# Routed attention with a greedy expert layer: the first unit's values handled behind its queries, keys and scores

## The chip, the cores and the metric

The kernel runs on one core of a Trainium2 chip. The metric is the time of one execution in microseconds on the device; the median of several runs counts. One execution was also recorded by the hardware profiler, and all rows below come from it.

## What is computed

An attention that is routed by clusters feeds a layer of eight experts. Queries and keys are each given the nearest of 16 centroids of their head, a query sees only keys of its own cluster, and the result goes through a greedy assignment of tokens to experts with a fixed capacity.

```python
# q, k, v: 4 batches x 8 heads x 768 x 64, float32; centroids 8 x 16 x 64
q_assign = np.argmax(np.einsum('bhsd,hcd->bhsc', q_n, c_n), axis=-1)   # likewise k_assign
mask = q_assign[:, :, :, None] == k_assign[:, :, None, :]
scores = np.where(mask, scale * np.matmul(q, k.transpose(0, 1, 3, 2)), -1e9)
attn = softmax(scores)
x = np.matmul(attn, v)                       # 3072 tokens x 512
logits = x @ w_gate                          # 8 experts, at most 384 tokens each
# greedy: the largest logit first, each token to one expert
out[mask_e] = np.maximum(x[mask_e] @ w1[e], 0) @ w2[e]
```

## The kernel before

The attention is cut into 8 units (u = 0 to 7), each of four heads of one batch. A head has 768 tokens, that is 6 blocks of 128, so a unit has 24 blocks. Queries, keys and values are float32 and are worked on as two float16 parts, a high and a low one. A unit passes through these stages:

- `load` (L481) fetches q, k or v over the queue of SP into one of four buffers `ld`, in turn. Unit 0 fetches q and k head by head (192 KB each) and v whole (768 KB); all later units fetch everything whole. Unit 2's keys use the buffer that unit 0's values had.
- `split_sc` and `split_hi` (L628, L632) scale and form the high part on ACT, and `split_lo` (L636) forms the low part by a subtraction on POOL or DVE. `dup` (L643) copies high parts on ACT.
- `pt` and `ptc` (L724, L736) transpose by PE and copy the result out on DVE or ACT (unit 0), `trans` (L720) does it by a DMA (later units).
- `cent0` and `cent` (L700, L662) multiply by the centroids on PE, into a PSUM tile called `mx`. `hh0` to `hh3` and `hot0` to `hot3` (L667) find the nearest on DVE, `hh4`/`hot4` and `hh5`/`hot5` (L683) form and place the marks on DVE and ACT. In unit 0 this is done head by head (`hh`).
- `vs` (L746) sums v over the tokens with 12 products on PE, into `mx` as well; `vact` and `vh2` (L754, L757) read it on ACT and `vl2` (L760) on DVE. The result is used from `av,u,1` on.
- `m_mm` (L766) forms a block of scores on PE and `m_rd` (L773) takes its row maximum on DVE. `row0` and `row1` (L786, L790) turn the maxima into two more rows.
- `b_mm`, `b_exp`, `res` and `av` (L804 to L826) are the second pass: scores again, the exponential on ACT, its low part on POOL, and the product with v on PE.

`wd` (L657) is a dummy product on PE whose result nobody reads. The pool of `mx` holds one tile, so each user of `mx` waits until the last reader of the user before has finished. The expert stage follows the last unit.

The order of all this is written out by hand: `ATT_ORDER` (L21) is a text of 2037 steps, and each engine, and the queue of SP, takes its instructions in the order in which they stand there. The scheduler of the framework adds only the waits that the data need. Around the change the text read in turn: `load,0,v` as the third load, v's three split steps among those of heads 1 and 2, `vs,0` behind the marks of head 1, `vact,0`, `vh2,0` and `vl2,0` among the dummies that follow, and `load,2,k` in front of `load,1,v` and `load,1,q`.

Of the kernel before, what the change touches and what calls it, by code (L numbers as in the profile page):

```python
# [21 lines left out]
ident loadc load,0,q,0 wtio load,0,k,0 misc load,0,v,- load,0,q,1 c0 load,0,k,1 c1 load,0,q,2 c2,0 c2,1 load,0,k,2 c2,2
c2,3 load,0,q,3 c2,4 zqb c2,5 split_sc,0,q,0 loadg c2,6 c2,7 load,0,k,3 split_sc,0,k,0 c2,8 c2,9 zkb load,1,k,- c2,10
split_hi,0,q,0,P split_hi,0,k,0,P split_sc,0,q,1 c2,11 split_lo,0,q,0,P split_sc,0,k,1 split_hi,0,q,1,P c2,12 pt,0,qa,0
split_hi,0,k,1,P split_lo,0,k,0,P ptc,0,qa,0,D split_sc,0,v,- c2,13 pt,0,ka,0 split_lo,0,q,1,P ptc,0,ka,0,D
split_hi,0,v,-,P c2,14 pt,0,qa,1 split_lo,0,k,1,P ptc,0,qa,1,D c2,15 dup,0,q,0 pt,0,ka,1 wgs c3 dup,0,k,0 c4
split_lo,0,v,-,P ptc,0,ka,1,D split_sc,0,q,2 cent0,0,k cent0,0,q split_sc,0,k,2 wd wd hh0,0 split_hi,0,q,2,P wd wd hh1,0
wd wd split_hi,0,k,2,P wd hh2,0 wd wd dup,0,q,1 hh3,0 wd wd wd hh4,0,k dup,0,k,1 wd hh4,0,q wd split_lo,0,q,2,P
load,2,k,- hh5,0,k cent0,1,k hh5,0,q pt,0,kb,0 split_sc,0,q,3 split_lo,0,k,2,P pt,0,qb,0 ptc,0,kb,0,D cent0,1,q
ptc,0,qb,0,A pt,0,qa,2 zqm hh0,1 pt,0,ka,2 hh1,1 split_sc,0,k,3 m_mm,0,0 tab,8 hh2,1 tab,9 wd split_hi,0,q,3,P tab,10 wd  # L30
hh3,1 wd tab,11 wd tab,12 split_hi,0,k,3,P wd hh4,1,k split_lo,0,q,3,P wd hh4,1,q wd hh5,1,k ptc,0,qa,2,D vs,0 hh5,1,q
split_lo,0,k,3,P ptc,0,ka,2,A m_rd,0,0 load,1,v,- dup,0,q,2 tab,13 pt,0,kb,1 load,1,q,- tab,14 pt,0,qb,1 tab,15 tab,16
ptc,0,kb,1,A pt,0,qa,3 tab,17 ptc,0,qb,1,D tab,18 wd wd tab,19 dup,0,k,2 tab,20 ptc,0,qa,3,D pt,0,ka,3 tab,21 tab,34
m_mm,0,1 split_sc,1,k,- tab,0 ptc,0,ka,3,D m_mm,0,2 m_rd,0,1 m_mm,0,3 wd wd wd dup,0,q,3 m_rd,0,2 m_mm,0,4 dup,0,k,3 wd
wd wd split_hi,1,k,-,P m_rd,0,3 m_mm,0,5 wd wd wd m_rd,0,4 m_mm,0,6 wd vact,0 wd split_lo,1,k,-,P wd vh2,0 m_rd,0,5
m_mm,0,7 split_sc,1,q,- wd wd wd vl2,0 m_mm,0,8 row0,0,0 cent0,2,k row1,0,0 cent0,2,q m_rd,0,6 split_hi,1,q,-,P wd wd wd
hh0,2 pt,0,qm,0 trans,1,ka,- hh1,2 wd wd split_sc,1,v,- split_lo,1,q,-,P wd hh2,2 wd wd hh3,2 wd wd wd hh4,2,k wd
hh4,2,q wd m_rd,0,7 hh5,2,k cent0,3,k hh5,2,q cent0,3,q split_hi,1,v,-,P wd hh0,3 pt,0,kb,2 hh1,3 wd wd ptc,0,kb,2,D wd
wd trans,1,qa,- wd ptc,0,qm,0,A wd split_lo,1,v,-,P hh2,3 wd wd hh3,3 wd wd wd hh4,3,k wd wd hh4,3,q hh5,3,k wd m_rd,0,8
wd hh5,3,q wd wd wd cent,1,k,0 tab,1 pt,0,qb,2 tab,2 tab,3 pt,0,kb,3 tab,4 ptc,0,qb,2,A pt,0,qb,3 ptc,0,kb,3,D  # L40
cent,1,k,1 load,2,q,- cent,1,k,2 ptc,0,qb,3,A tab,5 load,2,v,- cent,1,k,3 tab,6 tab,7 load,3,k,- m_mm,0,9 hot0,1,k
dup,1,k,- tab,22 m_mm,0,10 tab,23 m_mm,0,11 hot1,1,k wd wd wd m_rd,0,9 wd wd dup,1,q,- wd wd wd hot2,1,k m_mm,0,12 wd wd
hot3,1,k wd split_hi,2,k,-,D wd wd m_rd,0,10 wd wd wd wd wd hot4,1,k b_mm,0,0 m_rd,0,11 hot5,1,k cent,1,q,0 cent,1,q,1
b_exp,0,0 trans,1,kb,- cent,1,q,2 row0,0,1 cent,1,q,3 row1,0,1 split_hi,2,q,-,D m_rd,0,12 res,0,0,P pt,0,qm,1 wd wd wd
hot0,1,q m_mm,0,13 b_mm,0,1 ptc,0,qm,1,A hot1,1,q av,0,0 hot2,1,q b_exp,0,1 m_mm,0,14 m_rd,0,13 split_hi,2,v,-,D
res,0,1,P hot3,1,q m_mm,0,15 b_mm,0,2 m_rd,0,14 av,0,1 b_exp,0,2 hot4,1,q m_mm,0,16 m_rd,0,15 hot5,1,q vs,1 res,0,2,P
dup,2,k,- trans,1,qb,- m_rd,0,16 m_mm,0,17 b_mm,0,3 m_rd,0,17 vact,1 m_mm,0,18 vh2,1 av,0,2 b_exp,0,3 row0,0,2 row1,0,2
b_mm,0,4 m_rd,0,18 res,0,3,P pt,0,qm,2 b_exp,0,4 vl2,1 m_mm,0,19 tab,24 ptc,0,qm,2,A m_rd,0,19 m_mm,0,20 res,0,4,P
av,0,3 b_mm,0,5 m_rd,0,20 m_mm,0,21 b_exp,0,5 av,0,4 split_lo,2,k,-,D b_mm,0,6 dup,2,q,- m_mm,0,22 m_rd,0,21 res,0,5,P
trans,2,ka,- b_exp,0,6 m_rd,0,22 m_mm,1,0 m_mm,0,23 res,0,6,P av,0,5 m_rd,1,0 b_mm,0,7 m_rd,0,23 m_mm,1,1 b_exp,0,7  # L50
row0,0,3 load,3,q,- b_mm,0,8 res,0,7,P row1,0,3 m_rd,1,1 pt,0,qm,3 b_exp,0,8 out0,0,0 m_mm,1,2 out1,0,0 ptc,0,qm,3,A
res,0,8,P b_mm,0,9 out2,0,0,D m_rd,1,2 cent,2,k,0 hi0,0,0 m_mm,1,3 b_exp,0,9 cent,2,k,1 hi1,0,0 b_mm,0,10
split_hi,3,k,-,D m_rd,1,3 res,0,9,P av,0,6 av,0,7 tab,25 tab,26 b_exp,0,10 m_mm,1,4 split_lo,2,q,-,D av,0,8 b_mm,0,11
m_mm,1,5 b_exp,0,11 av,0,9 m_rd,1,4 res,0,10,P trans,2,qa,- cent,2,k,2 cent,2,k,3 m_rd,1,5 b_mm,0,12 res,0,11,P m_mm,1,6
hot0,2,k b_exp,0,12 av,0,10 m_rd,1,6 b_mm,0,13 res,0,12,P m_mm,1,7 hot1,2,k b_exp,0,13 av,0,11 load,3,v,- m_rd,1,7
b_mm,0,14 res,0,13,P m_mm,1,8 out0,0,1 b_exp,0,14 b_mm,0,15 out1,0,1 out2,0,1,D res,0,14,P m_mm,1,9 m_rd,1,8 hi0,0,1
b_exp,0,15 hi1,0,1 b_mm,0,16 split_hi,3,q,-,D m_rd,1,9 res,0,15,P xtr,0,0 av,0,12 av,0,13 hot2,2,k b_exp,0,16 m_mm,1,10
split_lo,2,v,-,D xst,0,0 av,0,14 b_mm,0,17 m_mm,1,11 b_exp,0,17 m_rd,1,10 res,0,16,P av,0,15 load,4,k,- m_rd,1,11
b_mm,0,18 res,0,17,P m_mm,1,12 b_exp,0,18 row0,1,0 av,0,16 row1,1,0 m_rd,1,12 rowt,1,0 b_mm,0,19 res,0,18,P m_mm,1,13
hot3,2,k b_exp,0,19 av,0,17 m_rd,1,13 b_mm,0,20 res,0,19,P m_mm,1,14 out0,0,2 b_exp,0,20 out1,0,2 b_mm,0,21 out2,0,2,D  # L60
row2,1,0 res,0,20,P m_mm,1,15 m_rd,1,14 hi0,0,2 b_exp,0,21 hi1,0,2 b_mm,0,22 m_rd,1,15 res,0,21,P av,0,18 b_exp,0,22
av,0,19 hot4,2,k m_mm,1,16 res,0,22,P tab,27 hot5,2,k tab,28 lg0,0,0 m_rd,1,16 av,0,20 trans,2,kb,- b_mm,0,23 lg1,0,0
split_lo,3,k,-,D m_mm,1,17 b_exp,0,23 cent,2,q,0 cent,2,q,1 cent,2,q,2 cent,2,q,3 m_rd,1,17 res,0,23,P av,0,21 b_mm,1,0
hot0,2,q trans,3,ka,- m_mm,1,18 b_exp,1,0 av,0,22 hot1,2,q b_mm,1,1 hot2,2,q res,1,0,P m_mm,1,19 m_rd,1,18 b_exp,1,1
av,0,23 hot3,2,q dup,3,k,- b_mm,1,2 res,1,1,P hot4,2,q m_mm,1,20 load,4,q,- m_rd,1,19 vs,2 hot5,2,q b_exp,1,2
trans,2,qb,- out0,0,3 out1,0,3 out2,0,3,D b_mm,1,3 vact,2 res,1,2,P m_rd,1,20 hi0,0,3 m_mm,1,21 b_exp,1,3 hi1,0,3
# [1393 lines left out]
```

## Time and profile before

| | |
|---|---|
| median of three runs | 711.02 us (708.17 to 711.4) |
| the profiled execution | 707.99 us, of which the span of the trace is 706.2 |
| PE busy (share of the span) | 659.0 us (93%) |
| DVE busy | 525.8 us (74%) |
| ACT busy | 425.2 us (60%) |
| POOL busy | 500.7 us (71%) |

PE is TensorE, DVE is VectorE, ACT is ScalarE, POOL is GpSimd, SP is the engine whose queue issues the transfers. Dummy products count as busy PE. The attention takes about the first 400 us. A timeline row gives the start in us, the duration in us, the engine, the line of the kernel, the operation, the tile written and the tiles read, the shapes, how many neighbours of the same kind are merged, and in brackets how long the engine had been idle before it and what ended that.

### The profile page before, as it was taken

To read this page: it belongs to the slowest core of one execution; us is meant where nothing else is said; L and a number is where in the kernel's file an instruction comes from. 1 tells how busy PE (TensorE), PEld (TensorE's weight loads), DVE (VectorE), ACT (ScalarE), POOL (GpSimd) and SP (SyncE) were. 2 spreads that over 40 slices of the span, in tenths; PEclk is the share of its full clock that TensorE was granted. 3 is DMA by queue.
4 is the path that set the end of the run, shared out by engine and by line. 5 is a ranking of instruction groups with operands and counts; after the bars stand their busy time and mean duration, and the time that the engine had idled before them with its cause. 6 is when DMAs were issued, how large, how long until landed. Compare 5 with 4: busy or idle time off the path is not lost. (4 is left out here: it accounts for less than half of the span.)

```text
span 706.2 us, 19751 instructions
## 1 busy us (share of the span) xinstructions
PE 659.0 (93%) x8256; PEld 438.0 (62%) x8256; DVE 525.8 (74%) x1149; ACT 425.2 (60%) x554; POOL 500.7 (71%) x395
## 2 busy tenths in 40 slices
...
GB/s 184 165 237 136 172 140 190 138 175 157 153 202 164 126 132 96 171 93 92 19 35 49 69 3 255 143 215 205 169 304 103 295 135 254 180 335 217 33 13 45
DMA packets 175451, 105.85 MB, mean 150 GB/s; under 512 B 135426, under 2 KB 160002, under 8 KB 175362
## 3 DMA queue, kind: packets, MB, share of 16 engines
...
q8 instruction: 64, 1.05, 0.6%
...
HBM read 58.77 MB, written 12.58 MB: 101 GB/s over the span
## 5 line engine op out<-in xcount | busy, mean ns | idle before, releaser
L824 POOL TENSOR_TENSOR rt<-pt 128x768 f16<-128x768 f32 x180 | 280.6, 1573 | 75.9 <-ACT pt L816 72.4
L816 ACT ACTIVATE pt<-sc 128x768 f32<-128x768 f32 x192 | 154.4, 811 | 121.2 <-PE sc L813 112.7
L774 DVE TENSOR_REDUCE mxs<-sc 128x1 f32<-128x768 f32 x192 | 180.9, 950 | 23.4 <-PE sc L770 20.1
L1382 PE MATMUL pf<-xgt,w1h 128*128 128x384 f16 (+1 forms) x640 | 128.8, 294 | 0.0
L835 PE MATMUL av<-vh,pt 128*128 128x66 f16 x1152 | 125.4, 195 | 2.3 <-DVE xb L868 1.9
L838 PE MATMUL av<-vh,rt 128*128 128x66 f16 x1152 | 125.0, 194 | 1.4 <-POOL rt L824 1.4
L837 PE MATMUL av<-vl,pt 128*128 128x64 f16 x1152 | 125.0, 192 | 0.0
L837 PEld LDWEIGHTS <-pt 128*128 128x128 bf16 x1152 | 106.6, 99 | 13.0 <-issue 4.0
L835 PEld LDWEIGHTS <-pt 128*128 128x128 bf16 x1152 | 107.4, 98 | 10.0 <-issue 0.3
L838 PEld LDWEIGHTS <-rt 128*128 128x128 f16 x1152 | 106.2, 97 | 1.6 <-POOL rt L824 1.6
L809 PE MATMUL sc<-qbt,kbt 99*128 99x384 f16 x384 | 94.8, 328 | 9.5 <-DVE mxs L774 8.9
L770 PE MATMUL sc<-kbt,qbt 80*128 80x384 f16 x384 | 93.2, 326 | 4.1 <-DMA qbt<-qb 2.0
L813 PE MATMUL sc<-qat,kat 128*128 128x384 f16 x384 | 94.5, 327 | 0.0
L1382 PE MATMUL pf<-xgt,w1l 128*128 128x384 f16 (+1 forms) x320 | 90.0, 294 | 0.0
L1344 ACT ACTIVATE wr<-wr 128x1024 f32<-128x1024 f32 x64 | 66.7, 1046 | 26.8 <-PE pc L1300 23.3
L1382 PEld LDWEIGHTS <-w1h 128*128 128x128 f16 x640 | 57.3, 97 | 28.4 <-ACT w2h L1347 0.7
L1420 PE MATMUL pf<-w2h,hh 128*128 128x512 f16 x192 | 72.7, 378 | 0.0
L1420 PE MATMUL pf<-w2l,hh 128*128 128x512 f16 x192 | 72.5, 378 | 0.0
L1420 PE MATMUL pf<-w2h,hl 128*128 128x512 f16 x192 | 72.5, 378 | 0.0
L1354 POOL TENSOR_TENSOR w2l<-wr,w2h 128x1024 f16<-128x1024 f32 x32 | 67.7, 2132 | 1.5 <-ACT w2h L1347 1.1
L1354 POOL TENSOR_TENSOR w1l<-wr,w1h 128x1024 f16<-128x1024 f32 x32 | 67.5, 2139 | 0.2
...
## 6 DMA issues: line engine op xcount, KB each, us to landing
...
xg<-xrow,idx POOLq DMA_INDIRECT x24, 6.3
```

The lines of the kernel that those rows point to most:

```text
L770: nc.tensor.matmul(p[:, half, :S // 2], QBT[u][:D + C, i, :], KBT[u][:D + C, h * J + half * 3:h * J + half * 3 + 3, :], start=True, stop=True)
L774: nc.vector.tensor_reduce(mxs[u % 3][:, i:i + 1], MP.pop((u, i))[:, :, :S // 2], axis=AX.XY, op=OP.max)
L809: nc.tensor.matmul(ps[:, half, :S // 2], KBT[u][:ER + 3, s, :], QBT[u][:ER + 3, cs, :], start=True, stop=False)
L813: nc.tensor.matmul(ps[:, half, :S // 2], KAT[u][:, s, :], QAT[u][:, cs, :], start=False, stop=True)
L816: nc.scalar.activation(pts[(u * 12 + s // 2) % RP][:, s % 2], MP.pop((u, "b", s))[:, :, :S // 2], AF.Exp, scale=ESC)
L824: (nc.vector if e == "D" else nc.gpsimd).tensor_sub(rts[x][:, s % 2], p.rearrange("p a b -> p (a b)"), hi_view(pts[x])[:, s % 2])
L835: nc.tensor.matmul(o[:, j, :], hi[:, js], VH[u][:, s, :], start=(kt == 0 and j == 0), stop=False, skip_group_check=True)
L837: nc.tensor.matmul(o[:, j, :D], hi[:, js], VL[u][:, s, :], start=False, stop=False, skip_group_check=True)
L838: nc.tensor.matmul(o[:, j, :], r[:, js], VH[u][:, s, :], start=False, stop=(kt == J - 1), skip_group_check=True)
L1354: nc.gpsimd.tensor_sub(lo, wrs[c], hi)
L1382: nc.tensor.matmul(o, (w1l if i == 2 else w1h)[x][:, c, fs], xgt[x][:, h + int(i == 1), ts], start=(first and i == 0), stop=(last and i == ...
L1420: nc.tensor.matmul(PS["o", p, g], (hl if i == 2 else hh)[x][:, f, g * P:(g + 1) * P], (w2l if i == 1 else w2h)[x][:, f, :], start=(f == 0 ...
```

## The change

No instruction is added or taken away; 9 of the 2037 steps stand elsewhere. `load,0,v` goes from the third place among the loads to behind `load,0,k,3`. `split_sc,0,v` and `split_hi,0,v` go from among the splits of heads 1 and 2 to behind `split_hi,0,k,3`, and `split_lo,0,v` to behind `split_lo,0,k,3`. `vs,0`, `vact,0`, `vh2,0` and `vl2,0` now stand together behind `hh4,3,q`, the marks of head 3, ahead of `hh5,3,k`, `m_rd,0,8` and `cent,1,k,0`. `load,2,k` goes behind `load,1,v` and `load,1,q`. All other steps, the dummies among them, keep their order. The lines of the text are wrapped anew, so the diff of the file is longer than the change; these are the places, with the wrapping taken out.

```diff
-... wtio load,0,k,0 misc load,0,v,- load,0,q,1 c0 load,0,k,1 ...
+... wtio load,0,k,0 misc load,0,q,1 c0 load,0,k,1 ...
-... c2,7 load,0,k,3 split_sc,0,k,0 c2,8 c2,9 zkb load,1,k,- ...
+... c2,7 load,0,k,3 load,0,v,- split_sc,0,k,0 c2,8 c2,9 zkb load,1,k,- ...
-... ptc,0,qa,0,D split_sc,0,v,- c2,13 pt,0,ka,0 split_lo,0,q,1,P ptc,0,ka,0,D split_hi,0,v,-,P c2,14 ...
+... ptc,0,qa,0,D c2,13 pt,0,ka,0 split_lo,0,q,1,P ptc,0,ka,0,D c2,14 ...
-... dup,0,k,0 c4 split_lo,0,v,-,P ptc,0,ka,1,D split_sc,0,q,2 ...
+... dup,0,k,0 c4 ptc,0,ka,1,D split_sc,0,q,2 ...
-... wd split_lo,0,q,2,P load,2,k,- hh5,0,k cent0,1,k ...
+... wd split_lo,0,q,2,P hh5,0,k cent0,1,k ...
-... tab,12 split_hi,0,k,3,P wd hh4,1,k split_lo,0,q,3,P wd hh4,1,q wd hh5,1,k ptc,0,qa,2,D vs,0 hh5,1,q
-split_lo,0,k,3,P ptc,0,ka,2,A m_rd,0,0 load,1,v,- dup,0,q,2 tab,13 pt,0,kb,1 load,1,q,- tab,14 ...
+... tab,12 split_hi,0,k,3,P split_sc,0,v,- split_hi,0,v,-,P wd hh4,1,k split_lo,0,q,3,P wd hh4,1,q wd hh5,1,k
+ptc,0,qa,2,D hh5,1,q split_lo,0,k,3,P split_lo,0,v,-,P ptc,0,ka,2,A m_rd,0,0 load,1,v,- dup,0,q,2 tab,13
+pt,0,kb,1 load,1,q,- load,2,k,- tab,14 ...
-... m_mm,0,6 wd vact,0 wd split_lo,1,k,-,P wd vh2,0 m_rd,0,5 m_mm,0,7 split_sc,1,q,- wd wd wd vl2,0 m_mm,0,8 ...
+... m_mm,0,6 wd wd split_lo,1,k,-,P wd m_rd,0,5 m_mm,0,7 split_sc,1,q,- wd wd wd m_mm,0,8 ...
-... hh4,3,k wd wd hh4,3,q hh5,3,k wd m_rd,0,8 wd hh5,3,q wd wd wd cent,1,k,0 ...
+... hh4,3,k wd wd hh4,3,q vs,0 vact,0 vh2,0 vl2,0 hh5,3,k wd m_rd,0,8 wd hh5,3,q wd wd wd cent,1,k,0 ...
```

## Rows read from the trace of the kernel before

**Rows 1.** Busy time of each engine and granted clock, one stretch of ten us.

```profile
core 0: us, PE busy (x) PEld busy (x) DVE busy (x) ACT busy (x) POOL busy (x), PEclk, DMA share, GB/s
20.00:30.00 10.00, 10.00 (x78) 6.33 (x77) 8.86 (x15) 9.16 (x16) 5.36 (x14) 1.00 0.52 165
```

**Rows 2.** Timeline: v's split on ACT and POOL.

```profile
start us, us, engine line op out<-in xcount [idle before <-releaser]
10.20 1.47 ACT L630 ACTIVATE ld<-ld 128x1536 f32<-128x1536 f32 x1
11.70 1.48 ACT L634 ACTIVATE vh<-ld 128x1536 f16<-128x1536 f32 x1
13.26 2.99 POOL L641 TENSOR_TENSOR vl<-ld,vh 128x1536 f16<-128x1536 f32 x1 [1.52 <-ACT vh L634]
```

**Rows 3.** Timeline, 7 to 18 us, four engines: what leads to the assignments.

```profile
7.72 0.91 POOL L641 TENSOR_TENSOR qa<-ld,qa 128x384 f16<-128x384 f32 x1
8.41 1.05 ACT L630 ACTIVATE ld<-ld 128x384 f32<-128x384 f32 x2 [2.36 <-DMA ld<-in_q_dram]
10.02 0.90 DVE L526 CAST cst<-sq 128x64 f16<-128x64 f32 x1
13.21 0.47 PE L653 MATMUL mx<-ct,kat 128*128 128x16 f16 x12 [0.38 <-DVE ct L549]
13.85 4.05 PE L660 MATMUL av<-wt,onesh 128*128 128x384 f16 x14
17.75 0.45 PE L653 MATMUL mx<-ct,kat 128*128 128x16 f16 x12
```

**Rows 4.** Timeline, 20 to 24 us: PE's dummies, ACT's splits, marks and copies.

```profile
20.12 1.30 PE L660 MATMUL av<-wt,onesh 128*128 128x384 f16 x7
20.45 0.51 ACT L634 ACTIVATE ka<-ld 128x384 f16<-128x384 f32 x1
21.15 0.28 ACT L691 ACTIVATE kb<-ceq 128x96 f16<-128x96 f16 x1 [0.19 <-DVE ceq L686]
23.20 0.81 ACT L732 ACTIVATE kbt<-sc 128x768 f16<-128x768 f16 x1 [0.49 <-PE sc L728]
```

**Rows 5.** Timeline: DVE's maxima, POOL's next subtraction, row0 twice.

```profile
25.07 4.40 DVE L774 TENSOR_REDUCE mxs<-sc 128x1 f32<-128x768 f32 x5
28.27 3.11 POOL L641 TENSOR_TENSOR ka<-ld,ka 128x1536 f16<-128x1536 f32 x1 [3.79 <-ACT ka L634]
30.02 1.39 DVE L788 TENSOR_SCALAR qm<-mxs 128x12 f16<-128x12 f32 x1
...
46.26 0.17 DVE L788 TENSOR_SCALAR qm<-mxs 128x12 f16<-128x12 f32 x1
```

**Rows 6.** Timeline: vl2 of unit 0; first product and vh2 of unit 1.

```profile
29.50 0.49 DVE L761 SCALAR_TENSOR_TENSOR vm<-vmh,rest,mx 2x256 f16<-2x256 f16 x1
...
53.68 0.27 PE L751 MATMUL mx<-vh,onesh 128*128 128x256 f16 x1
...
55.57 0.38 ACT L758 ACTIVATE vmh<-mx 2x256 f16<-2x256 f32 x1
```

**Rows 7.** Timeline, 35 to 42 us: dummies, head 3's marks, the second unit's assignment.

```profile
35.80 2.93 PE L660 MATMUL av<-wt,onesh 128*128 128x384 f16 x17
37.25 0.42 DVE L686 TENSOR_TENSOR ceq<-mx,cm 128x96 f16<-128x96 f32 x2
38.56 0.45 PE L653 MATMUL mx<-ct,kat 128*128 128x16 f16 x12
39.73 0.56 DVE L734 COPY kbt<-sc 128x768 f16<-128x768 f16 x1 [0.28 <-PE sc L728]
40.96 0.56 DVE L675 TENSOR_REDUCE cmx<-mx 128x24 f32<-128x384 f32 x1 [0.43 <-PE mx L653]
```

**Rows 8.** Timeline of SP's queue: the load of the third unit's keys.

```profile
16.27 0.38 SPq L488 DMA_DIRECT2D ld<-in_k_dram  x1
```

**Rows 9.** Busy time and granted clock in stretches of one us.

```profile
111.00:112.00 1.00, 0.00 (x0) 0.00 (x0) 0.54 (x2) 0.00 (x0) 1.00 (x2) 1.00 0.30 57
113.00:114.00 1.00, 1.00 (x5) 0.48 (x4) 0.56 (x1) 0.52 (x1) 0.00 (x0) 0.50 1.17 337
116.00:117.00 1.00, 1.00 (x18) 0.64 (x17) 0.75 (x2) 0.23 (x1) 0.59 (x1) 0.92 0.92 175
```

More of the change, by code (lines that the diff above doesn't have):

```diff
@@ L21 @@
 ATT_ORDER = """
[L22 to L66, printed above, removed]
@@ L67 @@
-b_mm,1,4 vh2,2 m_rd,1,21 res,1,3,P av,1,0 b_exp,1,4 av,1,1 vl2,2 split_hi,3,v,-,D tab,29 m_mm,1,22 res,1,4,P av,1,2
-m_rd,1,22 xtr,0,1 b_mm,1,5 split_hi,4,k,-,D m_mm,1,23 split_lo,3,q,-,D av,1,3 xst,0,1 b_mm,1,6 b_exp,1,5 av,1,4
+ident loadc load,0,q,0 wtio load,0,k,0 misc load,0,q,1 c0 load,0,k,1 c1 load,0,q,2 c2,0 c2,1 load,0,k,2 c2,2 c2,3
+load,0,q,3 c2,4 zqb c2,5 split_sc,0,q,0 loadg c2,6 c2,7 load,0,k,3 load,0,v,- split_sc,0,k,0 c2,8 c2,9 zkb load,1,k,-
+c2,10 split_hi,0,q,0,P split_hi,0,k,0,P split_sc,0,q,1 c2,11 split_lo,0,q,0,P split_sc,0,k,1 split_hi,0,q,1,P c2,12
@@ new lines @@
+m_mm,0,0 tab,8 hh2,1 tab,9 wd split_hi,0,q,3,P tab,10 wd hh3,1 wd tab,11 wd tab,12 split_hi,0,k,3,P split_sc,0,v,-
+split_hi,0,v,-,P wd hh4,1,k split_lo,0,q,3,P wd hh4,1,q wd hh5,1,k ptc,0,qa,2,D hh5,1,q split_lo,0,k,3,P
+split_lo,0,v,-,P ptc,0,ka,2,A m_rd,0,0 load,1,v,- dup,0,q,2 tab,13 pt,0,kb,1 load,1,q,- load,2,k,- tab,14 pt,0,qb,1
+tab,15 tab,16 ptc,0,kb,1,A pt,0,qa,3 tab,17 ptc,0,qb,1,D tab,18 wd wd tab,19 dup,0,k,2 tab,20 ptc,0,qa,3,D pt,0,ka,3
+tab,21 tab,34 m_mm,0,1 split_sc,1,k,- tab,0 ptc,0,ka,3,D m_mm,0,2 m_rd,0,1 m_mm,0,3 wd wd wd dup,0,q,3 m_rd,0,2 m_mm,0,4
@@ new lines @@
+dup,0,k,3 wd wd wd split_hi,1,k,-,P m_rd,0,3 m_mm,0,5 wd wd wd m_rd,0,4 m_mm,0,6 wd wd split_lo,1,k,-,P wd m_rd,0,5
+m_mm,0,7 split_sc,1,q,- wd wd wd m_mm,0,8 row0,0,0 cent0,2,k row1,0,0 cent0,2,q m_rd,0,6 split_hi,1,q,-,P wd wd wd hh0,2
+pt,0,qm,0 trans,1,ka,- hh1,2 wd wd split_sc,1,v,- split_lo,1,q,-,P wd hh2,2 wd wd hh3,2 wd wd wd hh4,2,k wd hh4,2,q wd
+m_rd,0,7 hh5,2,k cent0,3,k hh5,2,q cent0,3,q split_hi,1,v,-,P wd hh0,3 pt,0,kb,2 hh1,3 wd wd ptc,0,kb,2,D wd wd
+trans,1,qa,- wd ptc,0,qm,0,A wd split_lo,1,v,-,P hh2,3 wd wd hh3,3 wd wd wd hh4,3,k wd wd hh4,3,q vs,0 vact,0 vh2,0
```

34 lines of the change are left out of this document (added).

## The prediction

> **What bounds the kernel now.** The views were read in this order: the page's slices, the stretches of the first 140 us, the waits, and then the timeline of each engine from 0 to 60 us, because every step that moves lies there. The page's chain ends in an output transfer, which says nothing of the start. In the first 45 us no scores of the second pass are formed yet, and the work goes from one engine to the next in the written order. In the stretch 20 to 30 us DVE is busy for 8.86 of 10 us and ACT for 9.16 [rows 1]; PE's 10.00 there contains dummy products. So a step put in front of others on ACT or DVE in these 45 us delays what follows, and I see nothing later that waits for a fixed time: all later work hangs on these first scores. A delay that is left at 45 us reaches the end.
>
> **What is taken away in front.** ACT splits the whole of v (1.47 + 1.48 us) and POOL subtracts (2.99 us, after 1.52 us of waiting) between heads 1 and 2 [rows 2]. ACT also stood 2.36 us for head 1's queries, whose load was queued behind the 768 KB of v [rows 3]. With v behind, heads 1 to 3 are split earlier on ACT and POOL. I give nothing for it, because two other things hold the first scores. POOL starts head 0's subtraction only at 7.72, after its own fills, and DVE then works through copies and the centroids' chain until PE starts the first assignment at 13.21, released by DVE. Behind it PE runs 14 dummies from 13.85 for 4.05 us, to 17.90, and the next real product (17.75 in the view, as neighbours overlap) is the second head's assignment [rows 3]. PE takes its queue in order, so the splits could come 4 us earlier and this product would not. The bounds: the cast at 10.02 took 0.90 us and ended when POOL's subtraction did [rows 3]; without such waits some 0.5 us could be won, and with POOL now subtracting head after head without a pause another such wait of up to 0.4 us could come in. I take 0, between -0.5 and +0.4.
>
> **First charge: v's two ACT steps in front of head 1's marks.** They now stand behind head 3's last split (starts 20.45) and ahead of hh5,1 (kb's marks, 21.15) [rows 4]. ACT would have waited 0.19 us there. 20.45 + 0.41 (the spacing of such neighbours) + 1.47 + 1.48, less some 0.06 of overlap, puts hh5,1 at 23.75, +2.6. Queued behind it on ACT are the copies of the transposes; the one at 23.20 had waited 0.49 us for PE [rows 4], which is now filled: +2.6 - 0.6 = +2.0 from there on. PE waits for the marks too: its 7 dummies end at 21.42 [rows 4], the sum over v that followed (12 products) is gone, so it stands 2.6 us until 24.03 and then does the transposes that began at 22.67. DVE gets its copies 2.0 later and its five maxima (4.40 us from 25.07) run from 27.1 to 31.5 [rows 5].
>
> Next is row0. In the trace it took 1.39 us from 30.02, though the same operation took 0.17 at 46.26, and it ended at 31.41, just after POOL's subtraction for the second unit (28.27 + 3.11 = 31.38) [rows 5]. I read this as DVE held until POOL is done. That subtraction starts when ACT has split the second unit's keys, so it too is 2.0 later: 30.3 to 33.4. DVE arrives earlier relative to it, at 31.5, because vl2 (0.49 us) no longer stands in front, but is held until 33.4: **+2.0**. Were row0 not held, it would end at 31.7, +0.3. I take +2.0, since the one row with the same neighbours shows the hold. The Trainium skill ("GPSIMD Engine Reference", section "Key points") says that POOL shares its SBUF interfaces with DVE when DVE is in a two-port mode or reads two SBUF inputs; the trace agrees, 1.39 against 0.17 us, and by the rule the sum is the +2.0. POOL itself has room for v: it idles 3.79 us before 28.27 [rows 5], and its small fills only move into that.
>
> **Second charge: the sum over v between head 3's marks and the second unit.** vs,0 writes the one PSUM tile mx, so it must wait for hh4,3,q (ends 37.25 + 0.42 = 37.67), and cent,1,k,0, the next writer of mx, must wait for vl2,0. Before, cent,1,k,0 started at 38.56 without such a wait, 0.89 us after the marks, behind dummies [rows 7]. Of these 17 dummies 13 now stand before vs,0; at 2.93 / 17 us each they are over at about the time the marks are. The chain is priced by the second unit's: products from 53.68, vh2 (behind vact on ACT) from 55.57, over at 55.95; vl2 takes 0.49 us [rows 6]. That is 2.27 + 0.49 and some 0.15 of handing on = 2.9 us. With the +2.0: marks done at 39.7, vl2 done at 42.6, cent,1,k,0 at 42.65, +4.1. Behind it on PE are the transposes of heads 2 and 3. Behind vl2 on DVE stand the maximum m_rd,0,8 and 7 small table steps; DVE idled 0.28 us before the copy at 39.73 and 0.43 before the next dependent step at 40.96 [rows 7], which takes back 0.7 of its +5.0. So hot0,1,k starts at 45.2, **+4.2**. Bounds of this second part: +1.9 (the chain's bare durations less 0.89) to +2.6. vact and vh2 stand in front of hh5,3 on ACT, but it ends before cent,1,k,0 and adds nothing.
>
> **Edits at nothing.** load,2,k needs v's buffer. It was issued at 16.27 [rows 8], as POOL ended v at 13.26 + 2.99 = 16.25 [rows 2], and now goes behind load,1,v and load,1,q, when POOL ends v at about 26.8. Behind it on SP is the transpose of the second unit's keys, not ready before 33.4, and its own reader stands behind hot0,1,k. If that cover went, ACT would wait for the landing, as it did 2.36 us for head 1's queries [rows 3]. That transpose starts 2.0 later, and its reader cent,1,k,0 is 4.1 later. The dummies keep their number.
>
> **The sum.** The profiled execution took 707.99 us (span 706.2), 3.0 under the median of the runs shown, 711.02. By the profile the changed kernel takes 707.99 + 4.2 = 712.2; the same +4.2 on the median is **715.2 us**, which I give. 0.5% of it is 3.6 us, about what a measurement of this kernel can tell from no change.
>
> **The rivals.** *Only one charge counts.* If row0 isn't held, the marks of head 3 are 0.3 late, and the second chain gives 0.3 + 2.1 = +2.4, 713.4; if the second chain hides, +2.0, 713.0. For it: the +2.0 hangs on one hold. Against: both rows repeat the neighbours that the change keeps.
>
> *PE loses its clock as well.* PE did nothing in 111 to 112 us, the granted clock was 0.50 (1.2 of 2.4 GHz) in 113 to 114, and by 116 to 117 it was back to 0.92 [rows 9]. The new gap of 2.6 us from 21.42 is longer. Some 3.2 us at half clock cost up to 1.6 us: +5.8, 716.8. Against: 1.9 us of it at 28 to 32 lie under row0's hold, which absorbs a fall that comes directly behind the gap; a fall at the second gap would not be absorbed. The Trainium skill ("TensorE: Matmul & The Clock Gate", section "What's actually happening") has activity release the full clock and idling withdraw it; rows 9 agree, and it gives this case its chance.
>
> *Faster: POOL's queue sets the start.* Between heads 1 and 2 v cost POOL 1.52 + 2.99 = 4.5 us [rows 2]. If the first scores waited for heads 2 and 3, all would move up by it, and v would then lie in the idle time before 28.27 [rows 5]: 711.0 - 4.5 = 706.5. It decides at PE's first product after the dummies: if that starts with its data and not with the dummies' end. The rows speak against it, as 17.75 lies right at 17.90 [rows 3]. That the change does nothing is not among the rivals, as the order text is what issues the work.
>
> **How the numbers follow.** Forecast +4.2: 0.48. One charge, +2.0 to +2.4: 0.27. Both and the clock, +5.8: 0.15. Faster, -4.5: 0.10. The runs shown spread by 3.2 us, so of the forecast's share about 0.33 measures as slower by over 0.5% and 0.15 within; of one charge 0.03 and 0.24; of the clock case 0.14 and 0.01; of the faster case 0.08 as faster and 0.02 within. That makes slower 0.50, within 0.42, faster 0.08. The range leaves out the faster case and the upper end of the clock case: 709.5 (one charge, measured as low as the profiled run lies) to 718.5 (the clock case, 1.7 above it).
>
> **What would show it.** Right: 14 dummies still end near 17.9; hh5,1 near 23.7; a gap of 2 to 3 us on PE before the transposes of head 1's kb; row0 long again and over with POOL near 33.4; vl2,0 between hh4,3,q and cent,1,k,0, and that product near 42.6. Wrong: the first assignments well before 13, row0 at 0.17 us, cent,1,k,0 under 41, or the loss at 45 us gone by 100.

## The result and the profile after

| | before | changed |
|---|---|---|
| median of ten runs | 711.31 us (708.17 to 713.1) | 715.60 us (711.81 to 717.91) |
| ratio, with its 95% interval | | 1.0053 (1.0032 to 1.0075) |
| the profiled execution | 707.99 us, span 706.2 | 715.55 us, span 713.8 |

By the ratio the change costs 3.8 us, by the medians 4.3. The rows of the changed kernel follow in three stretches. The columns are those of the rows of before.

The timeline of the changed kernel from 7 to 20 us, to be read against [rows 3]: ACT's wait for head 1, POOL, DVE and PE.

```profile
7.10 0.52 ACT L630 ACTIVATE ld<-ld 128x384 f32<-128x384 f32 x1 [0.58 <-DMA ld<-in_k_dram]
...
12.14 0.91 POOL L641 TENSOR_TENSOR ka<-ld,ka 128x384 f16<-128x384 f32 x1
12.18 1.58 DVE L552 TENSOR_SCALAR wg<-wgf 128x32 f16<-128x32 f32 x1
12.99 0.59 POOL L567 MEMSET qm<- 128x600 f16 x1
13.91 0.28 DVE L549 COPY ct<-mx 128x256 f16<-128x256 f16 x1
14.24 0.47 PE L653 MATMUL mx<-ct,kat 128*128 128x16 f16 x12 [1.64 <-DVE ct L549]
14.88 4.64 PE L660 MATMUL av<-wt,onesh 128*128 128x384 f16 x14
19.32 0.51 PE L653 MATMUL mx<-ct,kat 128*128 128x16 f16 x12
```

ACT no longer stands 2.36 us for head 1. But the first assignment stands at 14.24, 1.03 later than in [rows 3]. DVE's scaling of the gate weights (the step `wgs`, L552) took 1.58 us while POOL went from the subtraction into a fill without a pause. The centroids' copy waited behind it on DVE, and PE for that copy (1.64). The dummies that follow took 4.64 us where they took 4.05, so in this execution the second head's assignment is 1.57 later.

The same timeline from 22 to 36 us, against [rows 4, 5]: the first charge.

```profile
22.04 1.30 PE L660 MATMUL av<-wt,onesh 128*128 128x384 f16 x7
...
22.79 1.47 ACT L630 ACTIVATE ld<-ld 128x1536 f32<-128x1536 f32 x1
24.29 1.48 ACT L634 ACTIVATE vh<-ld 128x1536 f16<-128x1536 f32 x1
25.68 0.27 ACT L691 ACTIVATE kb<-ceq 128x96 f16<-128x96 f16 x1
...
26.00 0.51 PE L728 MATMUL sc<-ident,kb 128*128 128x128 f16 x6 [2.66 <-ACT kb L691]
...
29.39 4.42 DVE L774 TENSOR_REDUCE mxs<-sc 128x1 f32<-128x768 f32 x5
32.19 3.12 POOL L641 TENSOR_TENSOR ka<-ld,ka 128x1536 f16<-128x1536 f32 x1 [1.28 <-ACT ka L634]
33.92 1.42 DVE L788 TENSOR_SCALAR qm<-mxs 128x12 f16<-128x12 f32 x1
```

v's two steps stand on ACT ahead of head 1's marks, PE waits 2.66 us for those marks, and row0 is long again: it ends at 35.34, POOL's subtraction at 35.31.

The same timeline from 39 to 48 us, against [rows 7]: the second charge.

```profile
39.66 2.28 PE L660 MATMUL av<-wt,onesh 128*128 128x384 f16 x13
41.19 0.42 DVE L686 TENSOR_TENSOR ceq<-mx,cm 128x96 f16<-128x96 f32 x2
41.77 0.27 PE L751 MATMUL mx<-vh,onesh 128*128 128x256 f16 x1
...
43.29 0.34 ACT L755 ACTIVATE mx<-mx 2x256 f32<-2x256 f32 x1 [2.51 <-PE mx L752]
...
44.08 0.49 DVE L761 SCALAR_TENSOR_TENSOR vm<-vmh,rest,mx 2x256 f16<-2x256 f16 x1 [2.47 <-ACT vmh L758]
44.62 0.44 PE L653 MATMUL mx<-ct,kat 128*128 128x16 f16 x12 [0.56 <-DVE vm L761]
...
47.03 0.56 DVE L675 TENSOR_REDUCE cmx<-mx 128x24 f32<-128x384 f32 x1 [0.30 <-PE mx L653]
```

The chain of the sum over v fills the time between head 3's marks and the second unit's first assignment, which is released by `vl2`. From the marks' end (41.61) to that assignment it is 3.01 us, where it was 0.89. `hot0,1,k`, DVE's first step on the second unit's keys, starts at 47.03, where it started at 40.96.

The granted clock of the changed kernel in single microseconds behind the first gap (columns: busy time and number of instructions of PE, PE's loads, DVE, ACT, POOL; granted clock; DMA share; GB/s).

```profile
26.00:27.00 1.00, 0.98 (x15) 0.86 (x16) 0.11 (x1) 1.00 (x3) 1.00 (x1) 1.00 1.04 390
27.00:28.00 1.00, 1.00 (x10) 0.66 (x9) 0.97 (x2) 1.00 (x3) 1.00 (x1) 0.58 1.07 399
28.00:29.00 1.00, 1.00 (x9) 0.81 (x8) 0.28 (x2) 1.00 (x2) 1.00 (x3) 0.50 1.07 390
...
30.00:31.00 1.00, 1.00 (x6) 0.51 (x5) 1.00 (x2) 0.91 (x3) 0.85 (x5) 0.72 0.55 106
31.00:32.00 1.00, 1.00 (x8) 0.60 (x7) 1.00 (x3) 1.00 (x1) 0.00 (x0) 1.00 1.01 381
```

Behind the gap of 2.66 us, in which PE did nothing, the granted clock fell to 0.50, which is 1.2 of 2.4 GHz; it fell between 27 and 28 us and was back at 1.00 by 31.

### The profile page after: what moved, and what is told of

Same layout as the page of the kernel before. It is cut to its first block, busy times and chain, and to the rows that moved or that the text cites. A ratio compares the mean times of both kernels' runs of the same rounds, so it can differ in the third digit from the quotient of the medians.

```text
span 713.8 us, 19752 instructions
## 1 busy us (share of the span) xinstructions
PE 660.9 (93%) x8256; PEld 438.4 (61%) x8256; DVE 525.5 (74%) x1149; ACT 424.7 (59%) x554; POOL 500.0 (70%) x395
```

## The experiments

Diffs of the order text show only the places, with the wrapping taken out. Where no other base is named, the base is the changed kernel. The front differs from one execution to the next, so the traces are also compared by the time from the second head's assignment (PE) to `hot0,1,k` (DVE): it is 23.21 and 23.50 us in two profiles of before, 27.71 and 27.33 in two of the changed kernel.

**One charge at a time: the sum over v put back.** `vact`, `vh2` and `vl2` stand where they stood before, and `vs` just ahead of `vact`; in the kernel before it stood further ahead, behind the marks of head 1. The splits of v stay late.

```diff
-... m_mm,0,6 wd wd split_lo,1,k,-,P wd m_rd,0,5 m_mm,0,7 split_sc,1,q,- wd wd wd m_mm,0,8 ...
+... m_mm,0,6 wd vs,0 vact,0 wd split_lo,1,k,-,P wd vh2,0 m_rd,0,5 m_mm,0,7 split_sc,1,q,- wd wd wd vl2,0 m_mm,0,8 ...
-... hh4,3,q vs,0 vact,0 vh2,0 vl2,0 hh5,3,k ...
+... hh4,3,q hh5,3,k ...
```

> The changed kernel, but with the sum over v (vs,0, vact,0, vh2,0, vl2,0) ahead of the centroids of heads 2 and 3, vact, vh2 and vl2 where they stood before and vs just ahead of vact. This leaves the front and the first charge and takes the second away. My theory (front 1.9, first charge 2.0, second 2.1 us): head 1's marks stay near 25.7 us, cent,1,k,0 starts near 42.5 and hot0,1,k near 44.9 instead of 47.0, and the time is some 2.1 us under the changed kernel's, about 2.2 over the kernel before. Rival (the sum hides behind the dummies where it stands now, and other waits end last): hot0,1,k stays within 0.5 us of 47.0 and the time stays at that of the changed kernel.

`hot0,1,k` stood at 44.64, near the 44.9 expected, PE and DVE:

```profile
18.42 0.52 PE L653 MATMUL mx<-ct,kat 128*128 128x16 f16 x12
...
44.64 0.56 DVE L675 TENSOR_REDUCE cmx<-mx 128x24 f32<-128x384 f32 x1 [0.18 <-PE mx L653]
```

But the second head's assignment, which lies ahead of every step moved here, stood 0.90 earlier than in the changed kernel's first profile (19.32). From it to `hot0,1,k` it is 26.22 us: 1.1 to 1.5 less than in the changed kernel, not 2.1. The median was 716.45 us, ratio 1.0075 (1.0052 to 1.0098), and no gain was seen in these four runs. So the same kernel was timed again, in twelve.

> The same kernel as the first experiment (the changed kernel with the four steps of the sum over v where they stood before), timed more often, since its four runs did not show the 2.1 us that its trace saved at 45 us (hot0,1,k at 44.64 where the changed kernel had 47.03 and 46.33). If that saving reaches the end, its ratio lies 0.002 to 0.003 under the changed kernel's 1.0053, at 1.002 to 1.0035. If the saving is given back later, it lies at 1.005 or above again, as its 1.0075 did.

713.35 us, ratio 1.0028 (1.0006 to 1.0049). All 16 runs together have a median of 713.9, some 2.7 us above the runs of before that were timed with them; the changed kernel lies 4.3 above. That points to a saving of 1 to 2 us at the end, about what the traces show, but the intervals overlap, so the times do not show it clear of the noise. The timeline of the second of these two, PE and DVE:

```profile
19.25 0.51 PE L653 MATMUL mx<-ct,kat 128*128 128x16 f16 x12
...
35.54 0.49 DVE L761 SCALAR_TENSOR_TENSOR vm<-vmh,rest,mx 2x256 f16<-2x256 f16 x1 [1.80 <-ACT vmh L758]
36.06 0.17 DVE L788 TENSOR_SCALAR qm<-mxs 128x12 f16<-128x12 f32 x1
...
45.78 0.56 DVE L675 TENSOR_REDUCE cmx<-mx 128x24 f32<-128x384 f32 x1 [0.18 <-PE mx L653]
```

From assignment to `hot0,1,k` it is 26.53 us here. The sum, now formed just ahead of where it is read, lets DVE wait 1.80 us for ACT ahead of row0 (1.50 in the other trace), and when row0 comes, POOL is done (35.32): it takes 0.17 us. It ends 16.68 and 16.98 us behind the second head's assignment, where it ended 13.66 and 13.95 behind it in the two profiles of before: +3.0, by another path than in the whole change. So this kernel does not show the first charge by itself.

**The other charge alone.** The kernel before, with only the four steps of the sum moved behind `hh4,3,q`.

```diff
-... wd hh5,1,k ptc,0,qa,2,D vs,0 hh5,1,q ...
+... wd hh5,1,k ptc,0,qa,2,D hh5,1,q ...
-... m_mm,0,6 wd vact,0 wd split_lo,1,k,-,P wd vh2,0 m_rd,0,5 ... wd wd wd vl2,0 m_mm,0,8 ...
+... m_mm,0,6 wd wd split_lo,1,k,-,P wd m_rd,0,5 ... wd wd wd m_mm,0,8 ...
-... hh4,3,q hh5,3,k ...
+... hh4,3,q vs,0 vact,0 vh2,0 vl2,0 hh5,3,k ...
```

> The kernel before with only the four steps of the sum over v moved behind the marks of head 3; loads and splits stay. My theory (second charge alone): the first assignment stays at 13.2 and row0 is long again and ends near 31; hot0,1,k starts at 42.6 to 43.1 instead of 40.96, the sum's chain of 2.9 us less 0.9 us of dummies that it replaces, less up to 0.5 us that PE wins at 21 us; the time is 1.6 to 2.1 us over the kernel before. Rival (the sum costs nothing there): hot0,1,k at 40.5 to 41.0 and no difference.

713.0 us, ratio 1.0024 (1.0004 to 1.0045). PE and DVE in this kernel:

```profile
19.22 0.45 PE L653 MATMUL mx<-ct,kat 128*128 128x16 f16 x12
...
38.12 0.42 DVE L686 TENSOR_TENSOR ceq<-mx,cm 128x96 f16<-128x96 f32 x2
41.02 0.49 DVE L761 SCALAR_TENSOR_TENSOR vm<-vmh,rest,mx 2x256 f16<-2x256 f16 x1 [2.47 <-ACT vmh L758]
41.56 0.44 PE L653 MATMUL mx<-ct,kat 128*128 128x16 f16 x12 [0.55 <-DVE vm L761]
...
43.97 0.56 DVE L675 TENSOR_REDUCE cmx<-mx 128x24 f32<-128x384 f32 x1 [0.31 <-PE mx L653]
```

Head 3's marks ended at 38.54 and the second unit's first assignment stood at 41.56, 3.02 later where it was 0.89: +2.1. `hot0,1,k` stood at 43.97, beyond the 42.6 to 43.1 expected, as the front ran late (the first assignment at 14.42, not 13.2). From the second head's assignment it is 24.75 us, only 1.4 more than before, since 12 products are gone from behind head 1's marks: head 3's marks end 19.32 us behind that assignment, where they ended 19.92 and 20.22 behind it.

So the kernel with the sum early carries +3.0 and this one +1.4, where the whole change carries +4.2. They nearly add up, and so do the ratios (1.0028, or 1.0075 in the first four runs, and 1.0024, against 1.0053), but at some 0.002 to either side the ratios prove no sum. Nor are these two the +2.0 and +2.1 of the prediction; those stand in the traces of the whole change itself.

**The step that stood long in front.** `wgs` goes from in front of the centroids' copy to behind head 0's marks, where POOL does nothing.

```diff
-... pt,0,ka,1 wgs c3 dup,0,k,0 c4 ...
+... pt,0,ka,1 c3 dup,0,k,0 c4 ...
-... hh4,0,q wd split_lo,0,q,2,P ...
+... hh4,0,q wgs wd split_lo,0,q,2,P ...
```

> The changed kernel with only the two small DVE steps of the gate's weights (wgs, L552 and L553) moved from ahead of c4 to behind hh4,0,q. In the changed kernel the first took 1.58 us from 12.18, while POOL subtracted without a pause, against 0.17 before. My theory (DVE is held by POOL's row of subtractions, and this delays the first assignment): the first assignment starts at 13.0 to 13.3 instead of 14.24, the second head's at 17.5 to 18.5 instead of 19.32, and hot0,1,k at 45.1 to 46.0; the time is 1 to 1.9 us under the changed kernel's. Rival (PE's clock sets the front, the dummies run at half rate until a fixed time): the first assignment moves as said, but the second head's stays at 19.0 to 19.4 and the time doesn't move.

714.06 us, ratio 1.0037 (1.0019 to 1.0054): by the medians 1.5 us under the changed kernel, though the intervals overlap. Its timeline from 12 to 46 us:

```profile
12.96 0.47 PE L653 MATMUL mx<-ct,kat 128*128 128x16 f16 x12 [0.38 <-DVE ct L549]
13.60 4.34 PE L660 MATMUL av<-wt,onesh 128*128 128x384 f16 x14
15.79 0.17 DVE L552 TENSOR_SCALAR wg<-wgf 128x32 f16<-128x32 f32 x1
17.78 0.45 PE L653 MATMUL mx<-ct,kat 128*128 128x16 f16 x12
...
45.10 0.56 DVE L675 TENSOR_REDUCE cmx<-mx 128x24 f32<-128x384 f32 x1 [0.31 <-PE mx L653]
```

`wgs` takes 0.17 us here, and the first assignment is 1.28 earlier than in the changed kernel. With the second head's assignment at 17.78, as in [rows 3], `hot0,1,k` stands at 45.10: +4.14 against [rows 7], and 27.32 us behind that assignment.

**Why row0 is long.** Three experiments. In the first, row0 gets another form, with a second input from SBUF (the constant -1/BIG as a tile).

```diff
-nc.vector.tensor_scalar(m, twice(u, cs), -(2.0 ** 29), -1.0 / BIG, op0=OP.max, op1=OP.mult)
+nc.vector.scalar_tensor_tensor(m, twice(u, cs), -(2.0 ** 29), cneg[...], op0=OP.max, op1=OP.mult)
```

> The changed kernel with row0 in another form: a scalar_tensor_tensor with a small constant tile as second tensor instead of a tensor_scalar with two constants; the numbers are the same. The two wgs steps show the forms side by side in the changed kernel: the tensor_scalar took 1.58 us and the scalar_tensor_tensor 0.19 while POOL was busy. My theory (row0 is held by POOL's subtraction because of its form): row0 takes about 0.2 us from 33.9, and hot0,1,k starts near 45.8 instead of 47.0; the time falls by about 1.2 us. Rival (row0 waits for its data, the maxima just in front of it): it takes 1.4 us again and hot0,1,k stays at 47.0.

715.98 us, ratio 1.0076 (1.0051 to 1.01), and row0 took 1.40 us from 33.85, not the 0.2 expected. So the long time isn't a matter of which of these two forms is used. By itself this also fits the rival, that row0 waits for the maxima in front of it; the third experiment decides that.

In the second, ACT's scaling of the second unit's queries was meant to go ahead of the high part of its keys. In the text, though, the high part went behind the low part's step, so that here the low part of the second unit's keys is formed from the first unit's high part; that part of the computation is changed.

```diff
-... wd wd wd split_hi,1,k,-,P m_rd,0,3 ... m_mm,0,7 split_sc,1,q,- wd ...
+... wd wd wd m_rd,0,3 ... m_mm,0,7 split_sc,1,q,- split_hi,1,k,-,P wd ...
```

> The changed kernel with ACT scaling the second unit's queries ahead of forming the high part of its keys, so that POOL's subtraction for the keys starts some 1.4 us later (near 33.6 instead of 32.2) and ends near 36.7. My theory (row0 is held until that subtraction ends, wherever it ends): row0 starts near 33.9 as before and takes 2.8 us, ending with POOL near 36.7, and hot0,1,k comes 1.3 to 1.5 us later. Rival (row0 waits for its data or has a price of its own): it takes 1.4 us again and hot0,1,k moves by less than 0.3 us.

714.8 us, ratio 1.0047 (1.0023 to 1.0072). POOL's subtraction came earlier and not later, 30.98 to 34.08, and row0 took 0.23 us from 33.88, to 34.11. The number expected did not come, since POOL moved the other way, yet row0 again ended with POOL.

The third is the one that was meant: only the scaling of the queries is moved.

```diff
-... wd wd wd split_hi,1,k,-,P m_rd,0,3 ... m_mm,0,7 split_sc,1,q,- wd ...
+... wd wd wd split_sc,1,q,- split_hi,1,k,-,P m_rd,0,3 ... m_mm,0,7 wd ...
```

> The changed kernel with one more step moved: ACT scales the second unit's queries (1.47 us) before it forms the high part of the second unit's keys, so POOL's subtraction for these keys starts 1.4 us later, at 33.6 where it started at 32.19, and ends at 36.7. DVE's way to row0 is not touched. If DVE's row0 is held by whatever subtraction POOL is in, it starts near 33.9 as before and takes some 2.8 us where it took 1.42, ending at 36.7, at most 0.05 us after POOL. If row0 is long for a reason of its own (its form, its place behind the maxima), it takes 1.4 us again and ends at 35.3. If POOL has not begun when row0 starts, it takes 0.17.

```profile
32.34 3.12 POOL L641 TENSOR_TENSOR ka<-ld,ka 128x1536 f16<-128x1536 f32 x1 [2.72 <-ACT ka L634]
33.00 2.49 DVE L788 TENSOR_SCALAR qm<-mxs 128x12 f16<-128x12 f32 x1
```

All of this stretch came 0.9 us earlier in this execution (718.29 us in one run), but against row0 the subtraction starts 1.07 later than in the changed kernel, and row0 is 1.07 longer: 2.49 us, over 0.03 after POOL. The times expected (33.9, 2.8 us, 36.7) did not come, but the relation did, and a price of row0's own of 1.4 us is out. In all traces of this case together:

| | row0 starts | takes | ends | POOL's subtraction ends |
|---|---|---|---|---|
| before, two profiles | 30.02, 31.79 | 1.39, 1.38 | 31.41, 33.17 | 31.38, 33.15 |
| changed, two profiles | 33.92, 33.69 | 1.42, 0.95 | 35.34, 34.64 | 35.31, 34.61 |
| sum late, alone | 30.46 | 1.83 | 32.29 | 32.25 |
| `wgs` later | 32.48 | 0.95 | 33.43 | 33.40 |
| other form | 33.85 | 1.40 | 35.25 | 35.22 |
| low part ahead | 33.88 | 0.23 | 34.11 | 34.08 |
| queries' scaling first | 33.00 | 2.49 | 35.49 | 35.46 |
| gap filled (below) | 32.67 | 2.28 | 34.95 | 34.92 |
| fills later, marks first (below) | 29.53, 29.01 | 1.39, 0.98 | 30.92, 29.99 | 30.88, 29.95 |
| sum early, two profiles | 34.93, 36.06 | 0.17, 0.17 | 35.10, 36.23 | 34.21, 35.32 |

Wherever POOL is still in its subtraction, row0 ends 0.02 to 0.04 us after it, whatever it takes for that; where POOL is done, it takes 0.17 us.

**The clock behind the first gap.** 16 more dummies in front of the transposes of head 1's marks keep PE at work.

```diff
-... m_rd,0,0 load,1,v,- dup,0,q,2 tab,13 pt,0,kb,1 ...
+... m_rd,0,0 load,1,v,- dup,0,q,2 tab,13 wd wd wd wd wd wd wd wd wd wd wd wd wd wd wd wd pt,0,kb,1 ...
```

> The changed kernel with 16 more dummies (0.163 us each at the full clock) ahead of the transposes of head 1's kb, in the gap of 2.66 us in which PE stands. In the changed kernel the granted clock fell behind this gap and the transposes took 0.85 us. My theory (row0 is held until POOL's subtraction ends, and this absorbs what the clock costs): the clock stays at full, the five maxima start up to 0.7 us earlier, but row0 again ends with POOL's subtraction and hot0,1,k moves by less than 0.3 us; the time is that of the changed kernel. Rival (the clock's fall is part of the loss): hot0,1,k comes 0.7 to 1.6 us earlier and the time falls by as much.

716.12 us, ratio 1.0074 (1.0048 to 1.01). The clock stayed at 1.00 from 20 to 31 us, and the maxima started at 28.16, 1.23 us earlier than in the changed kernel. Row0 then took 2.28 us, to 34.95. That is 15.67 us behind the second head's assignment (19.28), where it is 16.02 and 15.64 in the two profiles of the changed kernel: the hold took the gain. The maxima, and PE's next rows, which show what came instead:

```profile
28.16 4.41 DVE L775 TENSOR_REDUCE mxs<-sc 128x1 f32<-128x768 f32 x5
...
35.94 0.50 PE L729 MATMUL sc<-ident,qm 128*100 128x128 f16 x6 [1.74 <-DVE mxs L775]
36.27 3.30 PE L661 MATMUL av<-wt,onesh 128*128 128x384 f16 x10
```

The longer hold lets PE wait 1.74 us, and ten dummies then take 3.30 us where they took 1.79; the granted clock was 0.50 from 37 to 39 us. `hot0,1,k` stood at 47.94, 0.91 later than in the changed kernel, where a move of less than 0.3 was expected. The rival, a start that comes 0.7 to 1.6 earlier, is out.

**A second profile of each kernel.** The profiled execution of before, 707.99 us, lies below the fastest of its ten timed runs (708.17), so both kernels were profiled again, unchanged.

> The changed kernel once more, for a second profile: the start ran 6.1 us behind at 45 us in the first, though the median is only 4.3 us up. My theory (the written order sets the start, chance only where PE's clock returns): the first assignment again at 14.2, gated by wgs, hot0,1,k at 46 to 47.1, and the end of the 14 dummies differs by up to 1 us. Rival (the 1.9 us of the front are chance): the first assignment near 13.2 and hot0,1,k near 45.2.

> The kernel before once more, for a second profile; the first came from a run of 707.99 us, 3 us under the median. My theory: the start has chance of its own here too, as head 1's queries lie behind v's load: the first assignment at 13.2 to 14.4 and hot0,1,k at 41.0 to 42.3. The stretch from 100 to 185 us should differ from the first profile by 2 to 4 us where PE's clock falls. Rival (the start is the same in each run): hot0,1,k at 40.9 to 41.1, and the runs differ only later.

The kernel before, in this second profile (712.12 us), ACT, PE and DVE:

```profile
9.30 1.10 ACT L630 ACTIVATE ld<-ld 128x384 f32<-128x384 f32 x2 [3.71 <-DMA ld<-in_q_dram]
...
14.14 0.47 PE L653 MATMUL mx<-ct,kat 128*128 128x16 f16 x12 [0.38 <-DVE ct L549]
...
19.22 0.51 PE L653 MATMUL mx<-ct,kat 128*128 128x16 f16 x12
...
42.72 0.56 DVE L675 TENSOR_REDUCE cmx<-mx 128x24 f32<-128x384 f32 x1 [0.43 <-PE mx L653]
```

Head 1's queries landed later behind v (ACT waits 3.71 us, 2.36 in [rows 3]), so the front of the kernel before is no fixed time: its first assignment stood at 13.21 and 14.14, and at 14.42 in the kernel with the sum late, which has the same front. `hot0,1,k` at 42.72 lies 0.4 beyond what was expected. In the changed kernel (second profile, 710.68 us) the first assignment stood at 14.23, as expected, and then:

```profile
19.00 0.45 PE L653 MATMUL mx<-ct,kat 128*128 128x16 f16 x12
...
46.33 0.56 DVE L675 TENSOR_REDUCE cmx<-mx 128x24 f32<-128x384 f32 x1 [0.31 <-PE mx L653]
```

In this pair of executions the changed kernel ends 1.44 us ahead, though it is 3.61 behind at `hot0,1,k`. What turns this round lies between 100 and 185 us; the next section has it.

**A front without either wait.** The kernel before, with head 1's loads ahead of v's, a group of POOL's fills (`misc`) behind its subtractions for heads 0 and 1, and `wgs` behind head 0's marks. (The expectation calls `wgs` the sum of the centroids' squares; it is the scaling of the gate weights.)

```diff
-... load,0,k,0 misc load,0,v,- load,0,q,1 c0 load,0,k,1 c1 ...
+... load,0,k,0 load,0,q,1 c0 load,0,k,1 load,0,v,- c1 ...
-... split_lo,0,k,1,P ptc,0,qa,1,D c2,15 dup,0,q,0 pt,0,ka,1 wgs c3 ...
+... split_lo,0,k,1,P misc ptc,0,qa,1,D c2,15 dup,0,q,0 pt,0,ka,1 c3 ...
-... hh4,0,q wd split_lo,0,q,2,P ...
+... hh4,0,q wgs wd split_lo,0,q,2,P ...
```

> The kernel before with the loads of head 1 put ahead of v's load, POOL's fills behind its subtractions for heads 0 and 1, and the sum of the centroids' squares (the DVE step that stood 1.58 us in the changed kernel) behind head 0's marks; v's split and its sum stay early as in the kernel before. If POOL's fills and head 1's late queries set the first assignment, it stands at 11.5 to 12.5 (13.21 and 14.14 in the two profiles of the kernel before), and hot0,1,k at 39 to 41 (40.96 and 42.72): 0.5 to 2 us less time, ratio 0.997 to 0.999. If what counts is the end of the 14 dummies behind it at half clock, a part of the gain is left: second head's assignment at 16 to 17. The rival, that v's split on ACT then stands in front of head 1's splits and nothing comes earlier, gives 13 or later and ratio 1.000.

710.18 us, ratio 0.9982 (0.9962 to 1.0002). The first assignment stood at 12.28, the second head's at 17.21, 0.2 beyond what was expected, `hot0,1,k` at 40.45. Behind the marks `wgs` fell into v's subtraction:

```profile
14.24 2.99 POOL L641 TENSOR_TENSOR vl<-ld,vh 128x1536 f16<-128x1536 f32 x1
...
15.10 2.17 DVE L552 TENSOR_SCALAR wg<-wgf 128x32 f16<-128x32 f32 x1
17.30 0.85 DVE L553 SCALAR_TENSOR_TENSOR wg<-wgf,wg 128x32 f16<-128x32 f32 x1
```

Last, from that kernel: head 0's marks (`hh5,0`; the expectation calls them head 1's) ahead of two copies on ACT, three dummies later, v's subtraction and with it `load,2,k` behind head 2's subtraction, and `wgs` behind `tab,7`.

```diff
-... dup,0,k,0 c4 split_lo,0,v,-,P ptc,0,ka,1,D ...
+... dup,0,k,0 c4 ptc,0,ka,1,D ...
-... wd wd dup,0,q,1 hh3,0 wd wd wd hh4,0,k dup,0,k,1 wd hh4,0,q wgs wd split_lo,0,q,2,P load,2,k,- hh5,0,k cent0,1,k hh5,0,q ...
+... wd wd hh3,0 wd wd hh4,0,k hh5,0,k hh4,0,q hh5,0,q dup,0,q,1 dup,0,k,1 split_lo,0,q,2,P cent0,1,k ...
-... split_lo,0,k,2,P pt,0,qb,0 ...
+... split_lo,0,k,2,P split_lo,0,v,-,P load,2,k,- pt,0,qb,0 ...
-... tab,11 wd tab,12 split_hi,0,k,3,P ...
+... tab,11 wd tab,12 wd wd wd split_hi,0,k,3,P ...
-... tab,6 tab,7 load,3,k,- ...
+... tab,6 tab,7 wgs load,3,k,- ...
```

> The kernel of the experiment with the fills later, in which the first assignment stood at 12.28 but the second head's only at 17.21, behind 14 dummies of 4.46 us, with head 1's marks (hh5,0) on ACT at 16.46 behind head 2's splits and copies though DVE was done at 15.18, and with POOL in v's subtraction until 17.23. Here hh5,0 goes ahead of the two copies on ACT, three of the dummies go to the later row in front of the sum over v, v's subtraction goes behind head 2's on POOL, and the two steps of wgs that took 2.17 and 0.85 us on DVE go behind tab,7, where POOL has no subtraction. If these set the second head's assignment: marks at 15.6 to 15.8, that assignment at 16.2 to 16.6, hot0,1,k at 39.5 to 39.9 where it was 40.45, wgs at 0.17 and 0.2 us; 0.5 to 0.9 us less, ratio 0.997. The rival, that the sum over v then waits for v's later subtraction, or PE for its clock, gives it back: hot0,1,k at 40.4 or more and ratio 0.998 or above.

709.83 us, ratio 0.9979 (0.9959 to 1.0). The second head's assignment stood at 15.26, 1.95 us earlier still, but `hot0,1,k` at 40.27, only 0.18 earlier, and not at 39.5 to 39.9 as expected: what the front wins is mostly gone by then. The trace names one wait that the kernel with the fills later doesn't have: ACT stood 2.35 us, to 29.91, for the load of the second unit's queries. Whether that takes it was not tried. Both kernels have lower medians than before, and neither interval excludes no change.

## Why the prediction was right

The median came out at 715.60 us, where 715.2 was given.

**The first charge** (+2.0) was right in place and size. `hh5,1` stands 4.53 later than in [rows 4]; of that 1.93 is the later front (the copy of head 0's marks, kbt, at 20.51 where it was 18.58), and 2.6 is left, the number given. The gap on PE is 2.66 us (2.6 given). Row0 ends 16.02 and 15.64 us behind the second head's assignment in the two profiles of the changed kernel, 13.66 and 13.95 in those of before: +2.0. That POOL's subtraction held it is shown by the table: twelve traces end with POOL, whatever row0 takes. The Trainium skill ("SBUF — State Buffer", section "Who interferes with whom") calls the ports that VectorE shares with GpSimd an exclusive lock: a VectorE step in a two-port mode, which a `tensor_scalar` can enter, and a GpSimd step wait for each other for the whole instruction, and a VectorE step with two inputs in SBUF contends with a GpSimd step that reads SBUF. The trace agrees, with row0 at 1.42 us in one form and 1.40 in the other. The Trainium skill has reductions free of the lock. The trace agrees: the maximum at 35.33, inside POOL's next subtraction (35.26 to 38.37), took 0.94 us.

**The second charge** (+2.1 behind the first) was right: 3.01 us from marks to assignment where 2.95 was given, 3.02 where it is alone. The 13 dummies (of 18; [rows 7] has 17 of them in one row) were over about when the marks were (41.94 and 41.61).

**The sum.** From the second head's assignment to `hot0,1,k` the change costs +4.2, as predicted (27.71 and 27.33 us against 23.21 and 23.50). With the front as in [rows 3], it is +4.14 (`wgs` later). That a delay which is left there reaches the end was argued, and single executions do not show it: the first pair of profiles ends 7.6 us apart, the second 1.4 the other way. The kernels together bear it out, as the ratio roughly follows `hot0,1,k`: 40.27 goes with 0.9979, 40.45 with 0.9982, 40.96 and 42.72 are the kernel before, 43.97 goes with 1.0024, 45.10 with 1.0037, 45.78 with 1.0028, 46.31 (low part ahead) with 1.0047, 46.33 and 47.03 with 1.0053, 47.06 (other form) with 1.0076, 47.94 with 1.0074. Only the first four runs with the sum early (44.64, 1.0075) fall out of it. One slip in the working: the low end of the range, 709.5, should be 710.0 by its own words (713.0 less 3.0); nothing hangs on it.

**The front** (0, between -0.5 and +0.4) came out near its number by luck, as two terms that the prediction did not have nearly cancel. Head 1's queries behind v cost more in the two other traces with that front than in the profile that I read, where I took the wait for hidden: the first assignment stands at 12.96 without it, against 13.21, 14.14 and 14.42 with it, so its removal wins 1.0 us against the mean of the three. And `wgs` lost 1.28: I named "another such wait of up to 0.4 us", for the cast of 0.90 us, and the one that came was longer, since POOL went on without a pause. Together the first assignment moves from 13.92, the mean of the three, to 14.24. The sign that I named, dummies over near 17.9, was wrong: the second head's assignment stood at 19.32.

**Of the rivals**, the loss of the clock did come behind the first gap, and row0's hold took it, as the text had it; behind the second, where PE stood 0.56 us, the granted clock stayed at 1.00. That only one charge counts fell with the traces of the whole change, in which row0 is held and the chain stands between marks and assignment, both times. That POOL's queue sets the start fell with the first assignment, which came no earlier. The edit put at nothing did cost nothing: `load,2,k` was issued at 28.86, as POOL ended v (28.83), and the transpose behind it at 35.33, as POOL ended its next subtraction (35.31).

**What stays open.** The profiled execution of the changed kernel took 7.6 us more than that of before, and its start explains 6.1. The rest moves between 100 and 185 us. From the fourth reciprocal of the outputs (DVE, L848) to the tenth it is 73.0 us in the first profile of before and 75.3 in the second, 74.1 and 70.1 in those of the changed kernel, and between these and 76.7 in the ten other traces. In that stretch PE waits for transfers; the waits of PE from 104 to 186 us name one, in the changed kernel's first profile and then in the second of before (columns: engine, tile and line; what is waited for: total us, times, longest).

```profile
PE sc L809 <- DMA qbt<-mt: 3.1, 2, 2.8
```

```profile
PE sc L809 <- DMA qbt<-mt: 3.0, 1, 3.0
```

The longest of these is 1.6 us in the changed kernel's second profile, and it isn't among PE's waits in the first of before. It differs within one kernel as much as between the two, so I count it to the spread of 6.1 us over the changed kernel's ten runs. What sets these landings was not tried.
